# Attention feeding two mixture-of-experts layers: a chunk's normalized rows are stored in the chunk's own iteration

## The chip, the cores and the metric

The kernel runs on one core of a Trainium2 chip. The metric is the device time of one execution in microseconds (us). TensorE (PE), VectorE (DVE), ScalarE (ACT) and GpSimd (POOL) each work through their own queue in order; SyncE (SP) issues most of the transfers, also in order.

## The reference

Decayed linear attention runs over a sequence of 768 positions (2 batches, 8 heads, width 64), and its 1536 rows of 512 numbers go through two mixture-of-experts layers with 8 experts each. Cut to what matters here:

```python
for t in range(S):
    state = gamma * state + einsum('bhd,bhe->bhde', k[:, :, t], v[:, :, t])
    y[:, :, t] = scale * einsum('bhd,bhde->bhe', q[:, :, t], state)
x = y.transpose(0, 2, 1, 3).reshape(B * S, H * D)
logits = x @ w_gate
expert_idx = argmax(logits, axis=1)        # first layer: one expert per row
gate_w = softmax(logits)[expert_idx]
# each expert takes its rows in order, up to its capacity
out[i] = gate_w[i] * (relu(disp @ w1) @ w2)[expert_idx[i], pos[i]]
# second layer: rows are given to experts greedily by logit, 192 to an expert
out[mask] = relu(x[mask] @ w1[e]) @ w2[e]
```

## The kernel before, in words

Attention is computed in 12 chunks of 128 positions (NCH = 12; six per batch, NCB = 6), in a loop over j from 0 to 10 with chunk 11 written out behind it. The order of each engine's work is the order in which the code is written. One iteration j holds, in this order:

- the loads of k and v of chunk j+2 (`load_kv`, tile kv, L121) and of q and k transposed of chunk j+3 (`load_qk`, tile qk, L117), 512 KB each, on the SP queue. Each tile has three buffers, so a load waits until the chunk three before has been used up. In iterations 0, 1, 8 and 9 an expert weight tile is also asked for (`issue`, tile wst, L195, 512 KB, four buffers);
- `decay(j + 1)`: GpSimd multiplies k of chunk j+1 by powers of the decay (kv, L255; not for the last chunk of a batch) and q likewise (qd, L258; not for the first chunk of a batch);
- `values(j)`: TensorE forms the chunk's outputs from the running state U and qd (L279) and from the masked scores AM and v (L283); ScalarE copies them out as xT (L286), with positions along the free axis;
- `keep(j - 1)`, which the change moves (L328 to L340): from the sum of squares ss of a chunk's rows, three small VectorE steps (`pow2`, tile p, L229 to L232) make a power-of-two scale; ScalarE copies the rows from PSUM, scaled, into xo (L334); GpSimd adds a small number to the softmax sum se (g, L337), VectorE takes its reciprocal (L338), GpSimd writes the product with the inverse scale into the last column of xo (L339), and SP stores the tile to the DRAM tensor xd (L340, 256.5 KB);
- `place(j - 1, j - 2)`: positions of chunk j-1's rows within their experts (plc on TensorE, L346; jv and oa on VectorE, L350 and L353; ob on GpSimd, L355) and the slot numbers of chunk j-2 (`dispatch`, acc on VectorE, L372);
- in iterations 5 to 8 a load of a quarter of one expert's second weights (`wide_load`, tiles wbh and wbl, L184, 512 KB);
- `state(j)`: TensorE adds to the running state (ya, L296), VectorE scales it into U (L298); `scores(j + 1)`: TensorE (B, L265) and the mask multiply on VectorE (AM, L269);
- `rows_mm(j)`: TensorE turns xT into rows and adds the gate logits (tile R, L306). R has one PSUM buffer, so this matmul waits until the rows of chunk j-1 have been read, by xo last of all;
- `gate(j)`: on VectorE lg, m, dl, jv, rv, oh, ohs (L313 to L326), one behind the other; on ScalarE the squares (L319, which give ss) and the exponentials (L322, which give se);
- `fill(FT[j])`: that many weight splits. For each, ScalarE makes the high half of 512 columns of a weight tile (wah, L215) and VectorE the rest (wal, L220). When a tile of two splits is done, the next one is asked for on the SP queue.

In iteration 9 (NA = 9) the slots of chunks 0 to 8 are turned into row numbers idx, and at the start of iteration 10 GpSimd gathers the rows of two experts from xd (L393), which wait for the stores of chunks 0 to 8. The code for chunk 11 also transposes the first gathered rows (`x_split`, L409), stores the remaining chunks and gathers the rest. After it come the experts of both layers, whose lines the change does not touch. The number of splits per iteration is fixed:

```python
FT = (0, 2, 2, 2, 2, 2, 3, 1, 1, 1, 0, 0, 0, 0, 1, 0)
```

Of the kernel before, what the change touches and what calls it, by code (L numbers as in the profile page):

```python
# [89 lines left out]
def moe_chain(ctx, tc, qk, kv, wg, w1, w2, cap, wg2, w21, w22, mt, tq, tb, pv, out):  # L90
# [24 lines left out]
    def load_qk(j):  # L115
        QK[j] = qkv.tile([128, 2, KD, C], F32, name="qk")
        SP.dma_start(QK[j].rearrange("p a h t -> p (a h t)"), _dap(qk, j * 128 * 2 * DM, [[2 * DM, 128], [1, 2 * DM]]))  # L117

    def load_kv(j):
        KV[j] = qkv.tile([128, 2, H, D], F32, name="kv")  # L120
        SP.dma_start(KV[j].rearrange("p a h d -> p (a h d)"), _dap(kv, j * 128 * 2 * DM, [[2 * DM, 128], [1, 2 * DM]]))  # L121
# [58 lines left out]
    def wide_load(i, h):  # L180

        if not h:
            W["b", i] = [w16.tile([128, 4, DM], F32, name="wb" + x) for x in "hl"]
        SP.dma_start(W["b", i][h // 2][:, h % 2 * 2:h % 2 * 2 + 2],  # L184
                     _dap(w2, i * DM * F + h * 256 * DM, [[DM, 128], [128 * DM, 2], [1, DM]]))

    def issue():

        if not todo:
            return  # L190
        nm, i, h = todo.pop(0)
        src = ((w1, w2) if i < E else (w21, w22))[nm == "b"]
        kk, ff = ((KD, F), (KF, DM))[nm == "b"]
        st = wst.tile([128, 1024], F32, name="wst")
        SP.dma_start(st.rearrange("p (k f) -> p k f", k=kk // 4),  # L195
                     _dap(src, (i if i < E else (i + ROT) % E) * DM * F + h * DM * F // 4, [[ff, 128], [128 * ff, kk // 4], [1, ff]]))
        staged.append([st, nm, i, h, 0])

    def fill(n, need=None, pool=False):

        while staged:
            p = staged[0]
            st, nm, i, h, s = p
            if need is not None:
                if turn.index((nm, i)) > turn.index(need):
                    return
            elif n <= 0 or i > done[nm] + 3:
                return
            n -= 1
            if h == 0 and s == 0:  # L210
                W[nm, i] = tuple(w16.tile([128, 4096], F16, name="w" + nm + x)
                                 for x in "hl")
            o = h * 1024 + s * 512
            hi, lo = (t[:, o:o + 512] for t in W[nm, i])
            A.activation(hi, st[:, s * 512:(s + 1) * 512], AF.Copy, scale=WS)  # L215
            if pool:
                A.activation(st[:, s * 512:(s + 1) * 512], st[:, s * 512:(s + 1) * 512], AF.Copy, scale=WS)
                G.tensor_tensor(lo, st[:, s * 512:(s + 1) * 512], hi, OP.subtract)
            else:
                V.scalar_tensor_tensor(lo, st[:, s * 512:(s + 1) * 512], WS, hi, op0=OP.mult, op1=OP.subtract)  # L220
            p[4] += 1
            if p[4] == 2:
                staged.pop(0)
                issue()

    def pow2(ss, rows=128, k=1):

        t = wk.tile([128, 3, k], I32, name="p2" + str(k))
        V.tensor_scalar(t[:rows, 0], ss.bitcast(I32), 1, 0x7F800000, op0=OP.logical_shift_right,  # L229
                        op1=OP.bitwise_and)  # L230
        V.tensor_scalar(t[:rows, 1], t[:rows, 0], -1.0, float(193 << 23), op0=OP.mult, op1=OP.add)
        V.tensor_scalar(t[:rows, 2], t[:rows, 0], float(61 << 23), None, op0=OP.add)  # L232
        return t[:rows, 1].bitcast(F32), t[:rows, 2].bitcast(F32)
# [16 lines left out]
    def decay(j):  # L250

        c = j % NCB
        if c < NCB - 1:
            x = KV[j][:, 0]
            G.tensor_tensor(x, x, tkt[:, c, :, None].to_broadcast([128, H, D]), OP.mult)  # L255
        if c:
            QD[j] = wk.tile([128, KD, 128], F32, name="qd", tag="qT")
            G.tensor_tensor(QD[j], QK[j][:, 0], tqt, OP.mult)  # L258
# [15 lines left out]
    def values(j):  # L274
        b, c = divmod(j, NCB)
        p = ps.tile([128, KD, 128], F32, name="C1")
        for h in range(KD if c else 0):
            for s in range(2):
                P.matmul(p[s * 64:(s + 1) * 64, h, :], U[s * 64:(s + 1) * 64, h, :], QD[j][s * 64:(s + 1) * 64, h, :],  # L279
                         start=h == 0, stop=False, skip_group_check=True)  # L280
        for h in range(KD):
            for s in range(2):
                P.matmul(p[s * 64:(s + 1) * 64, h, :], KV[j][:, 1, 2 * h + s, :], AM[j][s][:, h, :],  # L283
                         start=not c, stop=True, skip_group_check=True)
        XT[j] = wk.tile([128, KD, 128], F32, name="xT")
        A.activation(XT[j], p, AF.Copy)  # L286
# [22 lines left out]
    def gate(j):  # L309

        pv = RW[j][:, :, :272].rearrange("p b (d c) -> p b d c", d=2)
        lg = wk.tile([128, E], F32, name="lg")
        V.tensor_reduce(lg, pv[:, :, :, 128:].rearrange("p b d e -> p e b d"), AX.XY, OP.add)  # L313
        m = wk.tile([128, 1], F32, name="m")
        V.tensor_reduce(m, lg, AX.X, OP.max)
        dl = wk.tile([128, E], F32, name="dl")
        V.tensor_scalar(dl, lg, m, None, op0=OP.subtract)
        ss = wk.tile([128, 1], F32, name="ss")
        A.activation(junk.rearrange("p (b d c) -> p b d c", b=2, d=2), pv[:, :, :, :128], AF.Square, accum_out=ss)  # L319
        ex = wk.tile([128, E], F32, name="ex")  # L320
        se = wk.tile([128, 1], F32, name="se")
        A.activation(ex, dl, AF.Exp, accum_out=se)  # L322
        V.scalar_tensor_tensor(jv, dl, 0.0, w8, op0=OP.is_ge, op1=OP.mult)
        V.tensor_reduce(rv[:, j:j + 1], jv, AX.X, OP.max)
        V.tensor_scalar(oh[:, j, :], w8, rv[:, j:j + 1], None, op0=OP.is_equal)
        V.tensor_tensor(ohs[:, j + 1, :], ohs[:, j, :], oh[:, j, :], OP.add)  # L326
        SS[j] = ss, se

    def keep(j):

        ss, se = SS[j]
        sc, inv = pow2(ss)
        xh = qkv.tile([128, XR], F32, name="xo", tag="g1")
        A.activation(xh[:, :DM].rearrange("p (b d c) -> p b d c", b=2, d=2),  # L334
                     RW[j][:, :, :272].rearrange("p b (d c) -> p b d c", d=2)[:, :, :, :128], AF.Copy, scale=sc)
        g = wk.tile([128, 1], F32, name="g")
        G.tensor_scalar(g, se, 1e-9, None, op0=OP.add)  # L337
        V.reciprocal(g, g)  # L338
        G.tensor_scalar(xh[:, DM:DM + 1], inv, OUT1, g, op0=OP.mult, op1=OP.mult)  # L339
        SP.dma_start(xd[j * 128:(j + 1) * 128, :], xh)  # L340
# [27 lines left out]
    def dispatch(j, sm):  # L368
        oa, ob = OH[j]
        for i in range(2):  # L370
            P.matmul(sm[:, i * E:(i + 1) * E], oa[:, i * 128:(i + 1) * 128], ob, start=True, stop=True)
        V.tensor_tensor(acc, acc, sm, OP.add)  # L372
# [18 lines left out]
    def gather(src, row, ix, key, e, i, n):  # L391
        t = qkv.tile([128, row], F32, name="xg", tag="g" + str(i))
        G.indirect_dma_start(out=t[:n], out_offset=None, in_=src,  # L393
                             in_offset=bass.IndirectOffsetOnAxis(ap=ix[:n, i * E + e:i * E + e + 1], axis=0))
        XG[key, i] = t
# [68 lines left out]
    for j in range(NCH - 1):  # L464
        if j + 2 < NCH:
            load_kv(j + 2)
        if j + 3 < NCH:
            load_qk(j + 3)
        if j in (0, 1, 8, 9):
            issue()  # L470
        decay(j + 1)
        if j == NA + 1:
            for e in range(2):
                gather(xd[:NA * 128, :], XR, idx, e, e, 0, 128)
        values(j)
        if j:
            keep(j - 1)
            place(j - 1, j - 2 if 1 < j != NA + 1 else None)
        if 5 <= j < 9:
            wide_load(0, j - 5)  # L480
        if j == NA:
            off = shift()
        state(j)
        scores(j + 1)
        if j == NA:
            dispatch(NA - 1, ps.tile([128, NQ], F32, name="dsp", tag="T", bufs=2))
            V.tensor_scalar(idx, acc, -1.0, 0.0, op0=OP.add, op1=OP.max)
        rows_mm(j)
        gate(j)
        fill(FT[j])  # L490
    j = NCH - 1
    values(j)
    x_split(0, (0, 128), tag="T")
    rows_mm(j)
    keep(j - 1)
    place(j - 1, j - 2)
    gate(j)
    l1(0, 0, 128, 0, 2, FT[11])
# [855 lines left out]
```

## Time and profile before

| | us |
|---|---|
| median of three runs | 472.17 |
| lowest, highest | 466.65, 477.76 |
| profiled execution | 465.31 |
| span of its profile | 463.5 |

The profile is one execution. Its span runs from the first instruction to the last; 1.8 us of the execution's time lie around it. Engine shares of the span: TensorE 88%, VectorE 66%, ScalarE 56%, GpSimd 27%. Rows of the timeline give the start, the duration, the engine and line, what is written from what, how many instructions a row merges, and in brackets how long the engine stood idle before it and on what. "SPq" is the SP queue's issue of a transfer.

### The profile page before, as it was taken

The page shows a single profiled execution, that of the slowest core. Times are in us where ns is not written, and L with a number is a line of the kernel's source. Part 1 is how long each engine was busy: PE and PEld are TensorE (multiplying, and loading weights), DVE is VectorE, ACT ScalarE, POOL GpSimd, SP SyncE. Part 2 cuts the span into 40 slices and gives each one's busy share as a digit, 9 for nine tenths or more (in the row PEclk, how much of TensorE's full clock was granted, in tenths as well). Part 3 has the DMA queues.
Part 4 walks back from the last instruction along what each step waited for, and adds up shares of the span by engine and source line. Part 5 has one row for each costly group of instructions (what it writes and reads, how often), then busy time and mean ns, then how long its engine had stood idle before and what let it go on. Part 6 is the DMA issues. An engine that isn't in the chain of part 4 may idle for free.

```text
span 463.5 us, 13188 instructions
## 1 busy us (share of the span) xinstructions
PE 407.4 (88%) x5398; PEld 383.2 (83%) x5398; DVE 304.9 (66%) x795; ACT 258.6 (56%) x571; POOL 124.2 (27%) x189
## 2 busy tenths in 40 slices
PE   6989688789899999999999769997899899999960
PEld 4767577789899999999999649997789789999960
DVE  2799787648789888878778666741279487872100
ACT  1345434447778786867866355331477677873310
POOL 1652544260020221302111056524111222111120
PEclk9899979999999999999999967999799999999995
DMA  9999996347899989888876435202178978971010
GB/s 202 395 313 266 367 330 212 134 150 248 283 292 289 311 275 285 259 293 269 268 245 188 128 112 181 92 3 59 69 250 272 299 236 297 302 240 36 24 49 5
DMA packets 42181, 98.83 MB, mean 213 GB/s; under 512 B 8896, under 2 KB 9280, under 8 KB 42112
## 3 DMA queue, kind: packets, MB, share of 16 engines
q1 hardware_dynamic: 35808, 84.31, 56.7%
q0 software_dynamic: 4608, 13.50, 9.1%
q8 instruction: 44, 0.72, 0.6%
q10 hardware_dynamic: 1696, 0.09, 0.4%
q14 instruction: 25, 0.20, 0.2%
HBM read 87.94 MB, written 9.95 MB: 211 GB/s over the span
## 4 chain that ended last, share of the span: by engine, by line
PE 52%; DVE 16%; DMA 15%; ACT 6%; issue 5%; POOL 2%; SPq 0%; POOLq 0%; ACTq 0%; DVEq 0%
DMA wst<-in_moe_w_dram 8%; PE T L440 7%; PE T L442 6%; PE T L441 6%; PE yps L551 6%; PE yps L550 6%; PE yps L552 6%; DVE wal L220 4%; DMA kv<-in_kv_dram 3%; DVE wbl L220 3%; PE xpt L409 3%; PE yps L546 3%; DMA xd<-xo 2%; ACT wbh L215 2%; DMA L<-yd 1%
## 5 line engine op out<-in xcount | busy, mean ns | idle before, releaser
L440 PE MATMUL T<-xsh,wah 128*128 128x216 f16 (+4 forms) x672 | 135.6, 233 | 4.6 <-DVE hl L457 2.8
L441 PE MATMUL T<-xsl,wah 128*128 128x216 f16 (+4 forms) x672 | 135.4, 233 | 0.0
L442 PE MATMUL T<-xsh,wal 128*128 128x216 f16 (+4 forms) x672 | 135.3, 233 | 0.0
L551 PE MATMUL yps<-hl,wbh 128*128 128x216 f16 (+3 forms) x544 | 116.0, 237 | 2.1 <-issue 1.7
L550 PE MATMUL yps<-hh,wbh 128*128 128x216 f16 (+3 forms) x544 | 116.0, 237 | 1.0 <-issue 1.0
L552 PE MATMUL yps<-hh,wbl 128*128 128x216 f16 (+3 forms) x544 | 116.0, 237 | 0.9 <-issue 0.9
L220 DVE SCALAR_TENSOR_TENSOR wal<-wst,wah 128x512 f16<-128x512 f32 x125 | 82.2, 702 | 16.7 <-ACT wah L215 13.5
L220 DVE SCALAR_TENSOR_TENSOR wbl<-wst,wbh 128x512 f16<-128x512 f32 x119 | 78.5, 698 | 15.7 <-ACT wbh L215 13.6
L215 ACT ACTIVATE wah<-wst 128x512 f16<-128x512 f32 x128 | 72.9, 622 | 8.6 <-DMA wst<-in_moe_w_dram 8.5
L215 ACT ACTIVATE wbh<-wst 128x512 f16<-128x512 f32 x120 | 69.3, 624 | 5.9 <-DMA wst<-in_moe_w_dram 5.9
L441 PEld LDWEIGHTS <-wah 128*128 128x128 f16 x672 | 66.0, 99 | 5.8 <-issue 5.5
L440 PEld LDWEIGHTS <-wah 128*128 128x128 f16 x672 | 66.1, 99 | 0.1
L442 PEld LDWEIGHTS <-wal 128*128 128x128 f16 x672 | 66.0, 99 | 0.0
L551 PEld LDWEIGHTS <-wbh 128*128 128x128 f16 x544 | 52.6, 98 | 3.0 <-issue 2.8
L552 PEld LDWEIGHTS <-wbl 128*128 128x128 f16 x544 | 52.6, 98 | 2.5 <-issue 2.3
L457 DVE SCALAR_TENSOR_TENSOR hl<-T,hh 128x432 f16<-128x432 f32 (+4 forms) x64 | 32.0, 502 | 33.2 <-ACT hh L451 32.3
L550 PEld LDWEIGHTS <-wbh 128*128 128x128 f16 x544 | 52.8, 99 | 0.7
L451 ACT ACTIVATE hh<-T 128x432 f16<-128x432 f32 (+4 forms) x76 | 32.9, 435 | 32.6 <-PE T L442 32.2
L583 POOL DMA_INDIRECT yd<-yr,sidx x16 | 16.5, 1032 | 118.3 <-ACT yr L635 90.6
L583 POOL DMA_INDIRECT out_dram<-orow,ixo x16 | 15.2, 951 | 99.3 <-ACT orow L1015 91.3
L570 ACT ACTIVATE yT<-yps 128x384 f32<-128x384 f32 (+2 forms) x20 | 7.9, 393 | 33.3 <-PE yps L552 21.5
L422 DVE TENSOR_TENSOR xsl<-xpt,xsh 128x432 f16<-128x432 f32 (+4 forms) x32 | 14.9, 498 | 15.5 <-ACT xsh L416 15.4
(256 smaller groups left out, 672.4 us busy)
## 6 DMA issues: line engine op xcount, KB each, us to landing
wst<-in_moe_w_dram SPq DMA_DIRECT2D x124, 512.0 KB
qk<-in_qk_dram SPq DMA_DIRECT2D x12, 512.0 KB
kv<-in_kv_dram SPq DMA_DIRECT2D x12, 512.0 KB
xd<-xo SPq DMA_DIRECT2D x12, 256.5 KB
wbh<-in_moe_w_dram SPq DMA_DIRECT2D x2, 512.0 KB
wbl<-in_moe_w_dram SPq DMA_DIRECT2D x2, 512.0 KB
pvt<-in_pv_dram SPq DMA_DIRECT2D x3, 192.0 KB
mt<-in_mt_dram SPq DMA_DIRECT2D x2, 256.0 KB
```

The costliest lines, as they stand in the source:

```text
L215: A.activation(hi, st[:, s * 512:(s + 1) * 512], AF.Copy, scale=WS)
L220: V.scalar_tensor_tensor(lo, st[:, s * 512:(s + 1) * 512], WS, hi, op0=OP.mult, op1=OP.subtract)
L422: V.tensor_tensor(lo, pd, hi, OP.subtract)
L440: P.matmul(p[:, s, c0:c1], wh[:, d, fs], xh[:, d, c0:c1], start=d == 0, stop=False)
L441: P.matmul(p[:, s, c0:c1], wh[:, d, fs], xl[:, d, c0:c1], start=False, stop=False)
L442: P.matmul(p[:, s, c0:c1], wl[:, d, fs], xh[:, d, c0:c1], start=False, stop=d == KD - 1)
L451: A.activation(hh, p[:, :, c0:c1], AF.Relu)
L457: V.scalar_tensor_tensor(hl, p[:, :, c0:c1], 0.0, hh, op0=OP.max, op1=OP.subtract)
L550: P.matmul(p[:, s, c0:n], wh[:, f, dsl], hh, start=f == 0, stop=False)
L551: P.matmul(p[:, s, c0:n], wh[:, f, dsl], hl, start=False, stop=False)
L552: P.matmul(p[:, s, c0:n], wl[:, f, dsl], hh, start=False, stop=f == KF - 1)
L583: w = G.indirect_dma_start(out=dst, out_offset=bass.IndirectOffsetOnAxis(ap=ap, axis=0), in_=src, in_offset=None)
```

## The change

`keep(j)` is called at the end of iteration j, between `gate(j)` and `fill(FT[j])`, for j from 0 to 10; before, `keep(j - 1)` was called in iteration j, behind `values(j)`, and for chunk 10 behind `rows_mm(11)`. `keep(11)` stays where it was.

```diff
         values(j)
         if j:
-            keep(j - 1)
             place(j - 1, j - 2 if 1 < j != NA + 1 else None)
...
         rows_mm(j)
         gate(j)
+        keep(j)
         fill(FT[j])
     j = NCH - 1
     values(j)
     x_split(0, (0, 128), tag="T")
     rows_mm(j)
-    keep(j - 1)
     place(j - 1, j - 2)
     gate(j)
```

On ScalarE, in the program's iterations 1 and 2 (R is the chunk's rows, p its scale, C the outputs of the chunk behind it, ind a scratch tile that takes the squares), before:

```order
L322 ACTIVATE ex,se<-dl 128x8
L215 ACTIVATE wah<-wst 128x512 x2
L286 ACTIVATE xT<-C_365 128x512
L334 ACTIVATE xo<-R_330,p_384 128x512
L319 ACTIVATE ind_155,ss<-R_428 128x512
```

and now:

```order
L322 ACTIVATE ex,se<-dl 128x8
L334 ACTIVATE xo<-R_330,p_350 128x512
L215 ACTIVATE wah<-wst 128x512 x2
L286 ACTIVATE xT<-C_376 128x512
L319 ACTIVATE ind_155,ss<-R_428 128x512
```

The scaled copy xo has moved ahead of both high halves wah and of the next chunk's xT.

On VectorE, at the end of iteration 1 (the scale steps p and the reciprocal g of chunk 1, then the splits):

```order
 L326 TENSOR_TENSOR ohs<-ohs,oh 128x8
+L229 TENSOR_SCALAR p_350<-ss 128x1
+L231 TENSOR_SCALAR p_350<-p_350 128x1
+L232 TENSOR_SCALAR p_350<-p_350 128x1
+L338 RECIPROCAL g<-g 128x1
 L220 SCALAR_TENSOR_TENSOR wal<-wst,wah 128x512 x2
-L229 TENSOR_SCALAR p_384<-ss 128x1
-L231 TENSOR_SCALAR p_384<-p_384 128x1
-L232 TENSOR_SCALAR p_384<-p_384 128x1
-L338 RECIPROCAL g<-g 128x1
 L372 TENSOR_TENSOR acc<-acc,plc 128x16
 L350 SCALAR_TENSOR_TENSOR jv,posv<-plc,oh 128x8
```

The four steps have moved from behind the splits to ahead of them.

On the queue of GpSimd, around iteration 2 (kv and qd are the decay multiplies of chunk 3, g and xo GpSimd's part of a stored row, ob a step of place), before:

```order
L255 TENSOR_TENSOR kv<-kv,tbt 128x512
L258 TENSOR_TENSOR qd<-qk,tqt 128x512
L337 TENSOR_SCALAR g<-se 128x1
L339 TENSOR_SCALAR xo<-p_384,g 128x1
L355 TENSOR_SCALAR ob<-oh,id_152 128x8
```

and now:

```order
L337 TENSOR_SCALAR g<-se 128x1
L339 TENSOR_SCALAR xo<-p_350,g 128x1
L255 TENSOR_TENSOR kv<-kv,tbt 128x512
L258 TENSOR_TENSOR qd<-qk,tqt 128x512
L355 TENSOR_SCALAR ob<-oh,id_152 128x8
```

Chunk 1's part of the row has moved ahead of chunk 3's multiplies. The SP queue keeps its cycle of store, wst, kv and qk, with the store of chunk j-1 where that of chunk j-2 stood ahead of the loads of iteration j.

## Rows read from the trace of the kernel before

**Rows 1.** Busy time by stage: PE, PEld, DVE, ACT, POOL, then PEclk, DMA share, GB/s.

```profile
20.00:45.00 25.00, 21.60 (x311) 18.57 (x308) 23.57 (x86) 12.88 (x33) 10.70 (x20) 1.00 1.00 302
45.00:73.00 28.00, 21.37 (x281) 18.37 (x281) 22.35 (x78) 12.10 (x31) 13.44 (x20) 0.88 1.01 346
```

**Rows 2.** The chain of waits, 33 to 45 us: start, us, what.

```profile
34.29 6.26 DMA kv<-in_kv_dram
...
40.69 1.05 POOL kv L255
...
43.65 0.28 POOL xo L339
...
44.20 5.06 DMA xd<-xo
```

**Rows 3.** Timeline: the matmul L306 of chunk 1 and of chunk 11.

```profile
20.76 1.19 PE L306 MATMUL R<-idw,xT 128*128 128x136 f32 x8
...
85.21 1.19 PE L306 MATMUL R<-idw,xT 128*128 128x136 f32 x8
```

**Rows 4.** Timeline, 33 to 40 us: gate, splits, scale steps and the next mask multiply.

```profile
33.47 1.28 DVE L269 TENSOR_TENSOR AM<-B,mt 128x512 f32<-128x512 f32 x2
33.49 1.28 POOL L258 TENSOR_TENSOR qd<-qk,tqt 128x512 f32<-128x512 f32 x1
...
34.66 0.18 DVE L313 TENSOR_REDUCE lg<-R 128x8 f32<-128x32 f32 x1
...
35.71 1.14 ACT L215 ACTIVATE wah<-wst 128x512 f16<-128x512 f32 x2
...
36.00 0.17 DVE L326 TENSOR_TENSOR ohs<-ohs,oh 128x8 f16<-128x8 f16 x1
36.36 1.29 DVE L220 SCALAR_TENSOR_TENSOR wal<-wst,wah 128x512 f16<-128x512 f32 x2 [0.19 <-ACT wah L215]
...
37.57 0.15 DVE L229 TENSOR_SCALAR p<-ss 128x1 int32<-128x1 int32 x1
37.76 0.15 DVE L231 TENSOR_SCALAR p<-p 128x1 int32<-128x1 int32 x1
...
37.95 0.69 ACT L334 ACTIVATE xo<-R,p 128x512 f32<-128x512 f32 x1 [0.61 <-DVE p L231]
37.96 0.15 DVE L372 TENSOR_TENSOR acc<-acc,plc 128x16 f32<-128x16 f32 x1
...
38.15 0.27 POOL L339 TENSOR_SCALAR xo<-p,g 128x1 f32<-128x1 f32 x1 [1.95 <-DVE g L338]
...
38.77 1.28 DVE L269 TENSOR_TENSOR AM<-B,mt 128x512 f32<-128x512 f32 x2
...
39.96 0.18 DVE L313 TENSOR_REDUCE lg<-R 128x8 f32<-128x32 f32 x1
```

**Rows 5.** Timeline: VectorE steps beside GpSimd's multiplies, at 23 and at 55 us.

```profile
22.77 1.13 DVE L323 SCALAR_TENSOR_TENSOR jv<-dl,w 128x8 f32<-128x8 f32 x1
...
54.69 3.81 DVE L220 SCALAR_TENSOR_TENSOR wal<-wst,wah 128x512 f16<-128x512 f32 x3 [0.20 <-ACT wah L215]
54.81 1.47 POOL L255 TENSOR_TENSOR kv<-kv,tbt 128x512 f32<-128x512 f32 x1 [2.96 <-DMA kv<-in_kv_dram]
...
56.25 1.71 POOL L258 TENSOR_TENSOR qd<-qk,tqt 128x512 f32<-128x512 f32 x1
```

**Rows 6.** Waits of VectorE, 0 to 95 us: us in total, times, longest.

```profile
DVE g L338 <- POOL g L337: 4.5, 2, 2.4
```

**Rows 7.** Timeline of L306 in iteration 6, and two windows (PEclk third from the end).

```profile
59.53 2.18 PE L306 MATMUL R<-idw,xT 128*128 128x136 f32 x8 [3.23 <-ACT xo L334]
...
58.00:59.00 1.00, 0.00 (x0) 0.00 (x0) 0.97 (x8) 0.21 (x1) 0.54 (x2) 0.73 0.96 360
...
65.00:66.00 1.00, 1.00 (x24) 0.69 (x22) 0.72 (x9) 0.48 (x1) 0.32 (x2) 0.85 1.05 367
```

**Rows 8.** Timeline of the SP queue: a kv load.

```profile
45.66 0.40 SPq L121 DMA_DIRECT2D kv<-in_kv_dram  x1
```

## The prediction

> **What bounds the kernel now.** Read the windows by stage first, then the chain of waits, then the timeline of single iterations. The change lies in the attention loop, which runs from about 15 to 88 us of the 463.5; what follows is a chain behind the gathers of its rows, so I take a shift of its end as a shift of the whole. From 20 to 73 us all three of VectorE, TensorE and the DMA engines look full: VectorE is busy 23.57 of 25.00 us in the first part and 22.35 of 28.00 in the second, the DMA share is 1.00 and 1.01 at 302 and 346 GB/s [rows 1]. The chain of waits goes from one kv load (6.26 us to landing) to GpSimd's multiply of it, to GpSimd's part of a stored row, and from there to the store [rows 2]. So the loop is tied to two things at once: a ring through VectorE and ScalarE, and a ring through the SP queue, where a kv load stands behind a store that itself needs GpSimd.
>
> The measure is the step from one row-turning matmul (L306) to the next. The first in full stride starts at 20.76 us, the last, of chunk 11, at 85.21 [rows 3]: ten periods in 64.45 us. The cleanest period is the one from lg at 34.66 to lg at 39.96, 5.30 us with two weight splits in it [rows 4]. 64.45 is 11 us more than ten of these. The surplus is made of VectorE waiting for GpSimd's multiplies [rows 5], of two reciprocals that wait for GpSimd's g (4.5 us in all, longest 2.4) [rows 6], and of a stretch at half clock [rows 7].
>
> **The change part by part.** No instruction is added or taken out. Per chunk move: three small VectorE steps and the reciprocal, one ScalarE copy (xo, 0.69 us), two GpSimd steps, and one store on the SP queue.
>
> *ScalarE and VectorE.* Until now ScalarE makes the splits' high halves (wah) while VectorE is still in the gate, so VectorE goes from the gate to wal after 0.19 us of waiting, and the p steps come behind. Now xo stands ahead of wah, and xo needs the p steps, which need the whole gate on VectorE's queue. Counted from the start of lg, by [rows 4]: the last gate step starts at 1.34 and takes 0.17, so p at 1.51; 0.19 to the second p, 0.19 on to xo: 1.89; xo 0.69: 2.58; from wah to the first wal 0.65: 3.23; two wal 1.21 (36.36 to 37.57): 4.44; acc to AM 0.81: 5.25; AM to the next lg 1.19: 6.44. That is 1.14 longer than 5.30. The cover that goes is the gate: wah ran beside it, and now VectorE stands idle from the reciprocal to 3.23. A period with one split is 0.61 shorter, 5.83, one with three 7.05; the period of iteration 10, with none, stays at 5.30. Iterations 1 to 5 have two splits, 6 has three, 7 to 9 one: 32.2 + 7.05 + 17.5 + 5.3 = 62.0 us without any waits for GpSimd.
>
> *What goes.* The matmul L306 no longer waits for xo, but its input xT now comes behind xo and both wah, so that is worth nothing by itself. The reciprocal no longer stands behind the next chunk's decay multiplies, and at iteration 10 no longer behind the two gathers: 4.5 us of stalls that the 62.0 does not contain. At the end, chunk 10's p steps and reciprocal leave the chain in front of the last gate: 0.39 (37.57 to 37.96 in [rows 4]).
>
> *GpSimd against VectorE.* This is the largest uncertain term. While GpSimd multiplies kv (1.05 us alone [rows 2]) or qd (1.28 [rows 4]), VectorE steps with both inputs in SBUF wait: three wal take 3.81 us instead of 3 times 0.61, a wait of 1.91 and a price of 0.96 where the small jv takes 1.13 instead of 0.17 [rows 5]. The mask multiply AM, 1.28 us, is not touched by a qd started 0.02 us behind it [rows 4]. In the new order GpSimd is free for the next multiplies after its part of the row, which starts 0.39 behind the second p (37.76 to 38.15) and takes 0.27 [rows 4]: 1.70 + 0.39 + 0.27 and 0.1 to the next, at about 2.45 after lg. If the load is there by then, kv runs to 3.5, holds the first wal by 0.26, and qd holds the second by its 1.28: 1.5 per pair. Six chunks (3, 4, 7 to 10) have the pair, three a single one (0.49 for the qd of chunks 5 and 11, 0.26 for the kv of chunk 6). Is the load there? The store goes out 0.55 after the start of GpSimd's part (43.65 to 44.20) [rows 2], the kv load 1.46 behind the store with two loads between, of which one now stands ahead of the store (44.20 [rows 2] to 45.66 [rows 8]), so about 1.0; it is issued 3.6 after lg, lands 6.3 [rows 2] to 9.1 us later (45.66 to the multiply at 54.81 [rows 5]) and so, with a period of 7, between 3 and 6 after the next lg. Partly it falls on wal, partly on AM, where it costs nothing. I take three quarters, 1.15 for a pair, which is near the lower row, and 0.9 for the singles: 6.9 + 0.9 = 7.8. The ends: nothing, and 1.91 for each pair with 1.24 for the singles, 12.7.
>
> The Trainium skill, "SBUF — State Buffer", Who interferes with whom, says that a VectorE step with two SBUF inputs and a GpSimd step that reads SBUF shut each other out for a whole instruction, and one with a single SBUF input is left alone. With the full 1.5 on six pairs and 1.24 for the singles that would be 10.2 instead of 7.8, and a result 2.4 us higher than mine. The trace agrees on wal (3.81) and on AM (1.28); what it can't show is where the multiplies fall in the new order.
>
> *The SP queue.* Each kv and qk load now stands behind the store of the chunk just gated, where before it stood behind that of the chunk before. The loads go out some 4 to 5 us later against the arithmetic, and the backlog of the DMA engines shrinks. In iterations 5 to 8 a chunk moves four loads of 512 KB and a store of 256.5, 2.36 MB, which at 346 GB/s [rows 1] takes 6.8 us, 27.3 for the four. My periods there are 25.2 without waits and about 30 with them, so the DMA engines bind only if the waits vanish; then 2.1 us come back. The ring through the queue (1.0 from store to kv load, up to 9.1 to landing, 2.3 of multiplies, about 1 for GpSimd's small steps, 0.55 to the next store but one) is 14.0 over two iterations, 7.0 each, just under my mean period of 7.2 with waits, so I put it at nothing.
>
> *Sum.* 62.0 + 7.8 = 69.8 against 64.45: 5.4 longer, less 0.39 at the end: **5.0 us slower**. Low end: 62.0 + 2.1 − 64.45 − 0.4, or 0.7 us faster. High end: 62.0 + 12.7 − 64.45 − 0.4, or 9.9 slower. The profiled execution took 465.31, so 470.3 in its place; the three runs have a median of 472.17, 6.9 above it, so I give 477.2 against that median.
>
> **The rivals.**
> *The waits hide.* The multiplies land under AM and the matrix work, and the stalls that go pay for the longer ring: −0.7 us, 471.5. For it: the qd in [rows 4] costs nothing, and a load that lands late moves its multiplies under AM. Against it: a late load delays the row's store, so the loads settle where they just arrive, and that is beside wal.
>
> *The clock falls again and again.* This one ends more than 2% slower. In the kernel before TensorE stood idle for 3.23 us before L306 at 59.53, and the granted clock was half of 2.4 GHz from about 58.4 to 65.3 us (0.73 in the slice from 58, 0.85 in that from 65) [rows 7]; L306 then took 2.18 instead of 1.19. TensorE has some 5.2 us of work in a period (42.97 of 53 us [rows 1], of a mean period of 6.45); in new ones of 7 or more it idles 2 to 2.6 us in every one, cut in two by the waits for U and for xT. If these pieces join to one as long as that before 59.53, the clock can fall in every second or third period. One fall costs, as an estimate, 1.7 us (6.9 us at half speed cost 3.5 us of its work, of which I count half as lying beside VectorE). Three falls are 5.2 on top of 5.0: 10.2 slower, 482.4; five are 13.6. Against it: TensorE's order puts the matmuls of values (L279, L283) between the two waits, so no piece should pass 2 us. It decides once a period's idling is one piece.
>
> **How the numbers follow.** Forecast 0.68, with a range of its own from 473 to 482; waits hidden 0.20; clock 0.12. The measurement can tell about 2%, 9.4 us. Slower by more: the clock's 0.12, and a twentieth of the forecast (all pairs at 1.91): 0.15. Faster by more would need the ring through xo not to be there: 0.03. Within 2%: 0.82. The range goes from 468 (hidden waits, and a median of runs that lie 11 us apart) to 485 (three or four falls of the clock).
>
> **What would show it.** Right: ten periods of L306 in about 70 us; wal starting 3.2 us behind lg, with ScalarE's wah behind xo, and VectorE's waits for wah of more than 1 us in each of nine periods instead of 0.19; the wait of the reciprocal for g gone. Wrong: wah beside the gate, or wal undisturbed in all periods (the hidden case), or a granted clock under 0.9 in several places between 20 and 75 us (the clock), or an unchanged start of the last L306 near 85.

## The result, and the profile after

The changed kernel is slower, by less than 2%: 474.22 us (median of 4 runs, 472.05 to 478.7) against 470.43 for the kernel before on the same chip (4 runs, 466.65 to 477.76), a ratio of 1.0114 with an interval of 1.0070 to 1.0159. That is 5.4 us (3.3 to 7.5) on 470.43. The ratio is of fast runs alone, so it is not quite that of the two medians, which stand 3.8 us apart. The forecast was 5.0 us slower, "within 2%", 477.2 us.

| | before | after |
|---|---|---|
| profiled execution, us | 465.31 | 474.18 |
| its span | 463.5 | 472.4 |
| L306 of chunk 1 and of chunk 11 start at | 20.76, 85.21 | 20.42, 92.67 |
| ten periods between them | 64.45 | 72.25 |
| the first nine of them (to chunk 10) | 58.88 | 66.72 |

The two profiled executions stand 8.9 us apart, more than the ratio says: that of before took 465.31, 5.1 below its own median, that of after stands at its median. A difference of one or two us between single executions is therefore not to be built on; one that a run with a single edit takes away again is.

Busy time by stage of the kernel after (the columns of [rows 1]; the loop is longer, so the second window ends later):

```profile
20.00:45.00 25.00, 20.88 (x278) 17.80 (x274) 20.56 (x70) 10.12 (x28) 11.21 (x16) 0.93 0.89 249
45.00:79.00 34.00, 23.46 (x311) 19.91 (x310) 27.09 (x93) 14.07 (x36) 16.34 (x23) 0.95 0.98 301
```

In [rows 1] VectorE was busy 23.57 of the first 25 us with 86 instructions; now it is 20.56 with 70, and the DMA share has fallen from 1.00 to 0.89. Neither is full any longer in this stretch. The matmuls that answer to [rows 3], from the timeline:

```profile
20.42 1.19 PE L306 MATMUL R<-idw,xT 128*128 128x136 f32 x8
...
92.67 1.09 PE L306 MATMUL R<-idw,xT 128*128 128x136 f32 x8
```

One iteration of the kernel after, 21 to 30 us, from lg to lg, to be held beside [rows 4]:

```profile
21.81 0.17 DVE L313 TENSOR_REDUCE lg<-R 128x8 f32<-128x32 f32 x1
...
23.59 0.69 ACT L334 ACTIVATE xo<-R,p 128x512 f32<-128x512 f32 x1 [0.64 <-DVE p L231]
...
23.79 0.27 POOL L339 TENSOR_SCALAR xo<-p,g 128x1 f32<-128x1 f32 x1 [0.53 <-DMA kv<-in_kv_dram]
...
24.14 1.04 POOL L255 TENSOR_TENSOR kv<-kv,tbt 128x512 f32<-128x512 f32 x1
...
24.18 1.14 ACT L215 ACTIVATE wah<-wst 128x512 f16<-128x512 f32 x2
...
24.83 2.58 DVE L220 SCALAR_TENSOR_TENSOR wal<-wst,wah 128x512 f16<-128x512 f32 x2 [1.14 <-ACT wah L215]
...
25.14 1.72 POOL L258 TENSOR_TENSOR qd<-qk,tqt 128x512 f32<-128x512 f32 x1
...
29.34 0.18 DVE L313 TENSOR_REDUCE lg<-R 128x8 f32<-128x32 f32 x1
```

ScalarE's wah, which in [rows 4] ran beside the gate, now comes behind xo, and VectorE stands idle for 1.14 us in front of wal, which starts 3.02 us behind lg. GpSimd's multiplies begin right behind its part of the row, so kv and qd run beside wal: two wal take 2.58 us where [rows 4] has 1.29. The chain of waits now runs through just these instructions up to 76.84 us, where it goes over to a weight load; one piece of it from 69 us on:

```profile
69.01 0.69 ACT xo L334
...
70.25 0.90 DVE wal L220
...
72.69 1.19 DVE AM L269 x2
...
75.60 0.69 ACT xo L334
```

The waits of the kernel after, 0 to 105 us (us in total, times, longest). The wait of the reciprocal for g, 4.5 us in [rows 6], is no longer among them:

```profile
DVE wal L220 <- ACT wah L215: 10.1, 9, 1.1
...
PE dsp L371 <- POOL ob L355: 3.2, 1, 3.2
...
PE xpt L409 <- DMA xg<-xd,idx: 1.8, 1, 1.8
```

The first is the forecast's, nine times. The other two are not in the forecast. That for ob makes the longest period, chunk 8 to chunk 9, 9.77 us. The timeline there:

```profile
77.78 1.13 POOL L255 TENSOR_TENSOR kv<-kv,tbt 128x512 f32<-128x512 f32 x1 [1.72 <-DMA kv<-in_kv_dram]
...
78.88 1.26 POOL L258 TENSOR_TENSOR qd<-qk,tqt 128x512 f32<-128x512 f32 x1
...
80.12 0.31 POOL L355 TENSOR_SCALAR ob<-oh,id 128x8 f16<-128x8 f16 x1
...
80.48 0.19 PE L371 MATMUL dsp<-ob,oa 128*128 128x8 f16 x2 [3.22 <-POOL ob L355]
...
80.53 2.02 PE L306 MATMUL R<-idw,xT 128*128 128x136 f32 x8
```

The kv load of chunk 10 is late; on GpSimd ob of chunk 8 stands behind the multiplies that wait for it; in iteration 9 TensorE needs this ob in front of L306 (the dispatch of chunk 8, on which the first gather's indices rest).

### The profile page after: what moved, and what is told of

Same layout as the page of the kernel before. It is cut to its first block, busy times and chain, and to the rows that moved or that the text cites. A ratio compares the mean times of both kernels' runs of the same rounds, so it can differ in the third digit from the quotient of the medians.

```text
span 472.4 us, 13182 instructions
## 1 busy us (share of the span) xinstructions
PE 410.3 (87%) x5398; PEld 384.6 (81%) x5398; DVE 310.1 (66%) x795; ACT 257.9 (55%) x571; POOL 128.0 (27%) x189
## 4 chain that ended last, share of the span: by engine, by line
PE 45%; DVE 21%; DMA 10%; issue 10%; ACT 8%; POOL 3%; SPq 0%; POOLq 0%; ACTq 0%; DVEq 0%
PE T L442 6%; PE T L440 6%; DMA wst<-in_moe_w_dram 6%; PE T L441 6%; PE yps L549 5%; PE yps L550 5%; PE yps L551 5%; DVE wal L220 5%; DVE wbl L220 4%; PE yps L545 2%; ACT wah L215 2%; PE xpt L409 2%; DVE AM L269 2%; DMA xg<-yd,ix 2%; DMA kv<-in_kv_dram 2%
## 5 line engine op out<-in xcount | busy, mean ns | idle before, releaser
L220 DVE SCALAR_TENSOR_TENSOR wal<-wst,wah 128x512 f16<-128x512 f32 x125 | 87.8, 745 | 28.1 <-ACT wah L215 24.6
L220 DVE SCALAR_TENSOR_TENSOR wbl<-wst,wbh 128x512 f16<-128x512 f32 x119 | 81.5, 724 | 17.3 <-ACT wbh L215 16.9
L319 ACT ACTIVATE ind<-R 128x512 f16<-128x512 f32 x12 | 7.2, 597 | 41.2 <-DVE lg L313 41.2
## 6 DMA issues: line engine op xcount, KB each, us to landing
xd<-xo SPq DMA_DIRECT2D x12, 256.5 KB
```

## The experiments

Three theories were set against each other. A: the scale steps and xo ahead of the splits hold up wah, and with it VectorE. B: the loads, which now stand behind the store of the chunk just gated, come late. C: the clock falls in the longer periods. All runs, each ratio against the kernel before in the same set of runs, and the loop as its profile shows it:

| kernel | ratio, interval | nine periods | ten |
|---|---|---|---|
| before | 1 | 58.88 | 64.45 |
| after | 1.0114, 1.0070 to 1.0159 | 66.72 | 72.25 |
| step behind the splits | 0.9965, 0.9918 to 1.0013 | 58.75 | 64.01 |
| store an iteration later | 1.0154, 1.0102 to 1.0205 | 62.68 | 70.97 |
| extra matmuls | 1.0077, 1.0036 to 1.0119 | 67.02 | 72.02 |
| after, no multiplies | – | 54.84 | – |
| before, no multiplies | – | 47.66 | – |
| after, ob early | 1.0129, 1.0062 to 1.0195 | 65.71 | 74.64 |
| step behind the splits, ob early | 0.9975, 0.9937 to 1.0013 | 60.18 | 64.86 |
| the same, gathers at once | 0.9929, 0.9880 to 0.9979 | 58.56 | 64.79 |
| the same, store later too | 0.9908, 0.9861 to 0.9955 | 53.29 | 64.36 |
| store later, gathers at once | 1.0030, 0.9991 to 1.0069 | 62.87 | 67.94 |
| before, g early | 1.0028, 0.9985 to 1.0071 | 61.61 | 66.10 |
| behind the splits, ob early, store later | 0.9861, 0.9819 to 0.9903 | 53.27 | 59.87 |

**The step behind the splits.** One line moves: everything stays in the chunk's own iteration, only the order against the splits is that of before.

```diff
         gate(j)
-        keep(j)
         fill(FT[j])
+        keep(j)
```

> The changed kernel with keep(j) still in its own iteration but behind the weight splits instead of ahead of them. If the splits pay (scale steps and xo ahead of wah): wal starts again about 1.7 us behind lg, the ten periods of L306 fall from 72.2 to 61 to 65 us, and the time is at or below that of the kernel before (ratio 0.98 to 1.00). If the loads pay (kv and qk behind the store of the chunk just gated): the store goes out later still, the periods stay at 70 to 74 and the ratio at 1.01.

Measured: ten periods 64.01 in place of 72.25, ratio 0.9965, with an interval that ends below where that of the changed kernel begins. From its timeline at 40 us, and the wait for ob that is left:

```profile
40.33 0.18 DVE L313 TENSOR_REDUCE lg<-R 128x8 f32<-128x32 f32 x1
...
41.38 1.14 ACT L215 ACTIVATE wah<-wst 128x512 f16<-128x512 f32 x2
...
42.03 1.29 DVE L220 SCALAR_TENSOR_TENSOR wal<-wst,wah 128x512 f16<-128x512 f32 x2 [0.19 <-ACT wah L215]
...
43.82 0.27 POOL L339 TENSOR_SCALAR xo<-p,g 128x1 f32<-128x1 f32 x1 [1.96 <-DVE g L338]
...
45.63 1.04 POOL L255 TENSOR_TENSOR kv<-kv,tbt 128x512 f32<-128x512 f32 x1 [1.54 <-DMA kv<-in_kv_dram]
...
73.87 0.19 PE L371 MATMUL dsp<-ob,oa 128*128 128x8 f16 x2 [3.72 <-POOL ob L355]
```

wal starts 1.70 behind lg, as in [rows 4]. A second thing is to be seen: GpSimd's part of the row (43.82) waits for VectorE's reciprocal, which stands with the p steps behind wal. So the multiplies, which stand behind it in GpSimd's queue, can't start before wal is over, and two wal take 1.29 us in each of the five periods that have two. The order of the two parts decides both what ScalarE does first and when GpSimd is let go. A holds.

**The store an iteration later.** The changed kernel, but the store is issued at its old place on the SP queue, behind the next iteration's loads.

```diff
+        if j < NCH - 1:
+            XH[j] = xh
+        else:
+            store(j, xh)
...
+    def store(j, xh):
         SP.dma_start(xd[j * 128:(j + 1) * 128, :], xh)
...
         if j:
+            store(j - 1, XH[j - 1])
             place(j - 1, j - 2 if 1 < j != NA + 1 else None)
...
     rows_mm(j)
+    store(j - 1, XH[j - 1])
     place(j - 1, j - 2)
```

> The changed kernel with the store alone issued at its old place on the SP queue, in the next iteration, so that the kv and qk loads stand ahead of it again; all else as changed. If the splits pay: ten periods of 69 to 72 us, the wait of the kv multiply for its load gone or small, ratio 1.005 to 1.012. If the loads pay: ten periods of 63 to 66, ratio about 1.00.

Measured: the waits of VectorE for wah are unchanged (10.1 us in 9), nine periods fall by 4.0 us to 62.68, but the last one takes 8.29 in place of 5.53, and the ratio is 1.0154, above what either theory gave, with an interval that overlaps that of the changed kernel. The timeline at the end of the loop shows what takes 2.8 of the 4.0 us back:

```profile
79.10 0.17 DVE L495 TENSOR_SCALAR idx<-acc 128x16 int32<-128x16 f32 x1
...
82.98 1.43 POOL L401 DMA_INDIRECT xg<-xd,idx  x1 [0.18 <-issue]
...
90.11 1.11 PE L417 MATMUL xpt<-idw,xg 128*128 128x128 f32 x4 [3.68 <-DMA xg<-xd,idx]
```

The indices are there at 79.10, the gather goes out 3.9 us later, behind GpSimd's g, its part of the row and the multiply of qd, and its rows reach TensorE 7.1 us after that. So B is a part of the loop's loss, and hardly of the total as long as the gathers stand where they do (the run with both edits, below, bears on this).

**Extra matmuls.** Eight warm-up matmuls behind each L306, so that TensorE has less idle time.

```diff
         rows_mm(j)
+        if j:
+            warm(8)
         gate(j)
```

> The changed kernel with eight idle matmuls (256 columns each, about 1.1 us, result unused) behind L306 in iterations 1 to 10, where TensorE otherwise waits. If the clock pays: no window under 0.9 between 20 and 90 us, ten periods of 67 to 69 us, 3 to 5 us back of the changed kernel's time. If the splits pay: the clock holds but the periods stay at 71 to 72, since VectorE sets them; a gain of 1 us or less.

Measured: ten periods 72.02, ratio 1.0077, which the intervals don't tell from 1.0114. Windows of this run:

```profile
25.00:50.00 25.00, 22.41 (x312) 18.83 (x309) 19.55 (x72) 11.18 (x30) 11.47 (x17) 1.00 0.80 237
50.00:80.00 30.00, 24.29 (x323) 20.25 (x321) 24.21 (x80) 12.99 (x34) 14.17 (x19) 1.00 0.97 302
```

The granted clock (third from the end) is 1.00 from 25 to 80 us. The seven periods from chunk 1 to chunk 8, which lie in this stretch but for the first 1.3 us, take 49.74 us; in the changed kernel, with two falls of the clock among them, they take 50.34. So these falls do not set the periods, and C is dropped as the cause of the loop's length. Later the clock falls here too (0.69 from 85 to 90 us), so the third fall of the changed kernel, from 80 us on, is not tested by this run. The added matmuls take some 1.04 us of TensorE's time in an iteration, beside VectorE's work; that they cost a little of what the clock gives back is not excluded.

**Without the decay multiplies, after and before.** A pair: both kernels without GpSimd's multiplies of kv and qd from chunk 3 on, so that only the order of the other work is left.

```diff
         c = j % NCB
+        if 3 <= j:
+            QD[j] = QK[j][:, 0]
+            return
         if c < NCB - 1:
```

> The changed kernel without GpSimd's decay multiplies from chunk 3 on (kv and q are used as loaded, so the rows, the routing and all times behind the attention loop are others; only the loop is read). By the sum of the prediction the periods without waits are 6.44 us with two splits, 7.05 with three, 5.83 with one: ten periods of about 62 to 63 us, wal 3.0 to 3.3 us behind lg, two wal in 1.3 us. If the loads pay instead, the periods stay near 72 us, with TensorE waiting for kv or qk.

> The kernel before without the decay multiplies of kv and qd from chunk 3 on (this part of the computation is left out, so only the attention loop is read and not the whole time). It is the partner of the changed kernel without the same multiplies, whose nine periods from chunk 1 to chunk 10 were 54.84 us. Theory A (the scale steps and the scaling of the row stand ahead of the weight splits and set the period wherever GpSimd does not): the same nine periods fall to about 45 us, some 1.1 us less in each, the first wal starts about 1.9 behind lg in place of 3.02, and xo no longer stands between lg and wah. Theory B (the loads, which stand behind the store of the chunk just gated, set the period): the loads of the kernel before are not behind that store, so its periods also fall, but the first wal would stand as late behind lg as before the change of order, and the sum would be limited by waits for kv. If neither holds, and the multiplies are what the change lengthens, the nine periods stay within 2 us of 54.84.

Measured: nine periods 54.84 (forecast 56.7) and 47.66 (expected some 45). The tenth (8.05 and 14.81), in which the gathers fall, is not read, since the rows and the routing are others in these two. One iteration of the changed order, then one of the order before, each from its timeline:

```profile
34.15 0.18 DVE L316 TENSOR_REDUCE lg<-R 128x8 f32<-128x32 f32 x1
...
35.94 0.69 ACT L337 ACTIVATE xo<-R,p 128x512 f32<-128x512 f32 x1 [0.64 <-DVE p L231]
...
37.17 1.29 DVE L220 SCALAR_TENSOR_TENSOR wal<-wst,wah 128x512 f16<-128x512 f32 x2 [1.14 <-ACT wah L215]
...
40.40 0.18 DVE L316 TENSOR_REDUCE lg<-R 128x8 f32<-128x32 f32 x1
```

```profile
34.00 0.18 DVE L316 TENSOR_REDUCE lg<-R 128x8 f32<-128x32 f32 x1
...
35.06 1.14 ACT L215 ACTIVATE wah<-wst 128x512 f16<-128x512 f32 x2
...
35.71 1.29 DVE L220 SCALAR_TENSOR_TENSOR wal<-wst,wah 128x512 f16<-128x512 f32 x2 [0.20 <-ACT wah L215]
...
39.30 0.18 DVE L316 TENSOR_REDUCE lg<-R 128x8 f32<-128x32 f32 x1
```

6.25 from lg to lg against 5.30, with wal 3.02 and 1.71 behind lg: the order alone costs 7.2 us in nine periods, and waits for loads have next to no part in it (one of 1.1 us, GpSimd's for a kv load, in the changed order). What the multiplies (with what waits for them) add on top is 66.72 − 54.84 = 11.9 after and 58.88 − 47.66 = 11.2 before. So in these two executions the whole difference, 7.84, is the order's 7.18 and 0.66 more. The multiplies cost about the same in both; they only stop other instructions.

**The kernel before with g early.** Only g (a small GpSimd step) and its reciprocal on VectorE, here `recip(j)`, move into the chunk's own iteration, behind the splits; the rest stays as before.

```diff
         gate(j)
         fill(FT[j])
+        recip(j)
```

> The kernel before with only g and its reciprocal moved into the chunk's own iteration, behind the splits; the scale steps, the row's scaling, its last column and the store stay an iteration later. The forecast counted the two waits of the reciprocal (4.5 us) as the one thing that the change removes. If that is right, the wait goes, ten periods fall from 64.45 to 60 to 62, and the ratio is 0.990 to 0.995. Rival (the wait is hidden by the GpSimd multiplies or followed by another wait for the same late load): the wait goes but ten periods stay within 1 us of 64.45, ratio 0.998 to 1.001.

Measured: no gain, ratio 1.0028, and ten periods of 66.10, longer than either expectation. VectorE's wait for g falls from 4.5 to 0.7 us. From the timeline:

```profile
31.73 1.04 POOL L255 TENSOR_TENSOR kv<-kv,tbt 128x512 f32<-128x512 f32 x1
...
31.83 3.18 DVE L220 SCALAR_TENSOR_TENSOR wal<-wst,wah 128x512 f16<-128x512 f32 x2 [0.19 <-ACT wah L215]
...
32.73 1.72 POOL L258 TENSOR_TENSOR qd<-qk,tqt 128x512 f32<-128x512 f32 x1
```

With g out of the way GpSimd goes from g straight to the multiplies, and these now stop wal (3.18 us for two). The 4.5 us of reciprocal waits were no loss that could simply be taken out: what stood behind the multiplies waited, what now stands beside them waits instead.

**ob early, in the changed kernel.** To price the wait that the forecast had not seen; `early_ob(j)` is GpSimd's ob of chunk j, which `place(j)` then uses.

```diff
         gate(j)
+        early_ob(j)
         keep(j)
```

> The changed kernel, with GpSimd's ob of a chunk computed in that chunk's own iteration, right behind the gate, where before it stood a full iteration later behind the multiplies. Theory (the missed term is the wait of TensorE for ob of chunk 8, behind the late multiplies of kv 10): the wait of dsp for ob (3.2 us) goes, the period from chunk 8 to chunk 9 falls from 9.77 to 6.5 to 7.0, the ten periods from 72.25 to about 69.3, and the whole time by 3 us, to a ratio of 1.003 to 1.008 with the kernel before. Rival (the late load of kv 10 holds this period in any case, through the multiply and what follows it): the period stays above 9 and the ratio at 1.011.

Measured: the period from chunk 8 to chunk 9 falls from 9.77 to 6.25, as expected, and the ratio is 1.0129: nothing is won. The period before it takes 9.64 in place of 7.52, beside a half-clock stretch (granted clock 0.82 in the window from 65 to 70 us, 0.50 from 70 to 75), and at the end of the loop TensorE waits 3.92 us for the gathered rows instead of 1.79. The expectation for the total failed; that these two follow from the wait that went, and are not one execution's luck, was not tested.

**ob early, with the step behind the splits.**

```diff
         gate(j)
-        keep(j)
         fill(FT[j])
+        early_ob(j)
+        keep(j)
```

> The changed kernel with the step placed behind the weight splits of its own iteration, and ob computed ahead of it. Theory: to the 64.01 us of ten periods that the step behind the splits gave, the removed wait for ob (3.7 us) gives back some 3 to 3.5, so ten periods of about 60.7 and a ratio of 0.988 to 0.992. Rival (what the wait hid is only uncovered: the load of kv 10 or the clock): ten periods stay above 63 and the ratio at 0.996.

Measured: ratio 0.9975 and ten periods 64.86, no gain over 0.9965 and 64.01; the rival had it right. The timeline shows the wait's successor:

```profile
73.54 1.04 POOL L255 TENSOR_TENSOR kv<-kv,tbt 128x512 f32<-128x512 f32 x1 [4.12 <-DMA kv<-in_kv_dram]
...
74.54 1.26 POOL L258 TENSOR_TENSOR qd<-qk,tqt 128x512 f32<-128x512 f32 x1
...
75.85 1.97 PE L279 MATMUL C<-qd,U 64*64 64x128 f32 x16 [3.60 <-POOL qd L258]
```

The load of kv 10 is late, and what waited for ob behind its multiply (3.72 us) waits now for qd behind it (3.60). At this one place the root is the load, as B has it.

**The gathers at once.** As the last, with the two gathers right behind idx in iteration 9, not in iteration 10 behind g, xo and qd.

```diff
         decay(j + 1)
-        if j == NA + 1:
-            for e in range(2):
-                gather(xd[:NA * 128, :], XR, idx, e, e, 0, 128)
...
             V.tensor_scalar(idx, acc, -1.0, 0.0, op0=OP.add, op1=OP.max)
+            for e in range(2):
+                gather(xd[:NA * 128, :], XR, idx, e, e, 0, 128)
```

> As the kernel before it in this call (step behind the splits, ob early), and the two gathers of the first expert are issued right behind idx in iteration 9, not an iteration later behind g, xo and qd on GpSimd. Theory (TensorE's wait for the gathered rows and the late start of the experts hang on the gathers' place on GpSimd): gathers within 1 us of idx, no wait of xpt for xg, the second gather of the experts 1 to 2 us earlier against the last row-turning matmuls, ratio 0.983 to 0.989. Rival (the gathers' 2 to 2.5 us on GpSimd delay g, xo and qd of the last iterations, and the experts start when the last chunk's store is done in any case): the last two periods grow by 1 to 2 us and the ratio stays within 0.002 of the kernel without this edit.

Measured: ratio 0.9929, between the two expectations, and by the intervals not told from the 0.9975 without this edit. TensorE no longer waits for the gathered rows, but the gather starts 5.4 us behind idx (75.17 to 80.56), not 1: for the last 3.42 of these GpSimd waits in it for the store of chunk 8, and g, xo and qd wait behind.

**The store later as well.** To take the late load away: the edits of the last kernel and the store at its old place on the SP queue, as in the run above.

```diff
         if j:
+            store(j - 1, XH[j - 1])
             place(j - 1, j - 2 if 1 < j != NA + 1 else None)
```

> The step behind the weight splits of its own iteration, ob early, the gathers right behind idx, and the store of a chunk's rows issued an iteration later, behind that iteration's loads. Theory B for the end of the loop (the loads that queue behind the store come 4 to 5 us later, and the one of kv 10 then ends the wait of iteration 9 or 10, whichever instruction stands behind it): kv 10 is no longer waited for, the step that without this edit took 8.8 to 11 us near chunk 9 or 10 falls to 6 to 7, nine periods from 58.6 to 60.2 down to about 55, and the ratio with the kernel before to 0.978 to 0.986. Rival (the DMA engines are full from 45 to 80 us in any case, so the place in the queue decides nothing): nine periods stay at 58 or more and the ratio at 0.993.

Measured: kv 10 is not waited for any more, the period from chunk 8 to 9 is 5.25 and nine periods are 53.29, better than expected (this profiled execution took 469.47, the median is 467.27). But the last period takes 11.07, and the ratio is 0.9908, not the 0.978 to 0.986 expected. The timeline names the cause:

```profile
75.79 1.19 POOL L406 DMA_INDIRECT xg<-xd,idx  x1 [6.94 <-DMA xd<-xo]
...
79.65 1.27 POOL L258 TENSOR_TENSOR qd<-qk,tqt 128x512 f32<-128x512 f32 x1
```

GpSimd stands 6.94 us in the gather until the store of chunk 8 has landed, and qd of chunk 11, which TensorE needs (it waits 5.28 us), stands behind.

**The old split order with both later edits.** The changed kernel, step ahead of the splits, with the gathers at once and the store later, its line as in the last diff.

```diff
             V.tensor_scalar(idx, acc, -1.0, 0.0, op0=OP.add, op1=OP.max)
+            for e in range(2):
+                gather(xd[:NA * 128, :], XR, idx, e, e, 0, 128)
         rows_mm(j)
         gate(j)
         keep(j)
         fill(FT[j])
```

> The changed kernel (the step ahead of the weight splits) with the gathers right behind idx and the store issued an iteration later, behind the loads. Theory A says that what is left against the kernel before is the place of the scale steps and of the row's scaling ahead of the splits: nine periods at about 62 to 63, some 4 us more than the kernel before's 58.88, the last period back at 5.5 to 6 in place of 8.29, and a ratio of 1.004 to 1.010. Rival (the loads and the gathers carry most of the 1.1%): nine periods at 59 or less, ratio 1.000 or below.

Measured: nine periods 62.87, as A has it, the last 5.07; the ratio is 1.0030, just under the 1.004 expected, with an interval of 0.9991 to 1.0069. Loads and gathers carry a part of the 1.1%, then; in the first nine periods the old order still costs 9.6 us against the four-place kernel above (53.29), which also has ob early.

**Three places.** The kernel with the four edits, with the gathers back at their place in iteration 10, behind qd.

```diff
         decay(j + 1)
+        if j == NA + 1:
+            for e in range(2):
+                gather(xd[:NA * 128, :], XR, idx, e, e, 0, 128)
...
             V.tensor_scalar(idx, acc, -1.0, 0.0, op0=OP.add, op1=OP.max)
-            for e in range(2):
-                gather(xd[:NA * 128, :], XR, idx, e, e, 0, 128)
```

> As the kernel with four places changed, but the two gathers are back at their place in iteration 10, behind the last multiply of qd: the step behind the splits, ob early, the store behind the next iteration's loads. Theory (GpSimd's wait of 6.9 us for the store of chunk 8, with g, xo and qd behind it, was what the early gathers cost there): qd of chunk 11 is ready before C asks for it, the last period falls from 11.07 to 8 or less, nine periods stay at 53 to 54, the gathers start at once behind idx's last releaser without a wait for the store of over 1.5 us, and the ratio with the kernel before is 0.980 to 0.988. Rival (the store's landing sets the end of the stage wherever the gathers stand): the first matmul that takes gathered rows starts no earlier against chunk 1 than in the four-place kernel, and the ratio stays at 0.989 to 0.993.

Measured: as expected in each point, and 1.4% faster than the kernel before, with an interval (0.9819 to 0.9903) below one and below that of the change: 462.11 us against 467.69, ratio 0.9861. In its timeline the gather no longer waits for the store, and two of the last matmuls of the loop stand at:

```profile
73.92 1.19 POOL L406 DMA_INDIRECT xg<-xd,idx  x1 [0.18 <-issue]
...
78.97 0.91 PE L422 MATMUL xpt<-idw,xg 128*128 128x128 f32 x4 [2.65 <-DMA xg<-xd,idx]
...
79.68 2.02 PE L306 MATMUL R<-idw,xT 128*128 128x136 f32 x8
```

With L306 of chunk 1 at 19.81 us that is ten periods of 59.87, 4.6 us less than in the kernel before. Its DMA share is 1.01 from 20 to 45 us, and its granted clock 1.00 from 15 to 75. Whether it needs ob early was not run.

## Why the prediction was right, and where it was off

*The mechanism.* Right in each of its points. wah stands behind xo; wal starts 3.02 us behind lg (forecast 3.23); VectorE waits for wah in nine periods, 10.1 us in all, 1.12 each on average, where the forecast had over 1 us in each (one of them, with three splits, was 0.93); the reciprocal's wait is gone; ten periods came out longer, 72.25 for "about 70". That it is the order against the splits is shown by the run that undoes it alone, 64.01, and by the pair without multiplies, 7.2 us apart.

*The ScalarE and VectorE term.* 56.7 us for the first nine periods (five of 6.44, one of 7.05, three of 5.83); 54.84 without multiplies. The single periods fit: three of the two-split periods took 6.26, the three-split one 7.04, two of the one-split ones 5.65 and 5.61. The error is mostly in the first, 5.38: L306 of chunk 1 starts 1.32 us ahead of its lg and the later ones 2.20, so this period is 0.9 shorter, though from lg to lg it has 6.26 as well.

*GpSimd against VectorE.* The mis-sized term: 7.8, against 11.9 measured. It counts the multiplies of chunks 3 to 11, which stand beside the splits of iterations 1 to 9, so all of it falls in the first nine periods. What was measured has two parts. 3.3 is the period from chunk 8 to 9 (9.77 against 6.46 without multiplies), which is no stop of VectorE (wal takes 0.69 there) but TensorE's wait for ob. The other 8.6 lie in eight periods. There my three quarters give 6.65 (7.8 less the 1.15 of one pair), and the full price gives 8.7 (five pairs of 1.5, and the singles' 1.24). So the full price comes out in sum, mine was too low, and the wait for ob was missing altogether. (The wait of three wal, 1.91, is right against the 1.90 that three take without multiplies; "3 times 0.61", as the forecast writes, is 1.83.) That VectorE and GpSimd stop each other, as the Trainium skill has it ("SBUF — State Buffer", Who interferes with whom), this trace agrees with on both sides: at 24.83 two wal took 2.58 in place of 1.29 with kv and qd beside them, and that qd 1.72 in place of 1.28.

*What goes.* "4.5 us of stalls that the 62.0 does not contain" is true of the sum, yet as a gain by itself it was not to be had: with g early and nothing else, the same multiplies stop wal, and the ratio is 1.0028.

*The SP queue.* "So I put it at nothing" is the step that did not hold. That the loads come later was right, but it was averaged over the ring. The store's place is worth 4.0 us in the nine periods of the changed kernel (62.68 with the store later), spread over them: only 1.3 fall on the period from chunk 8 to 9 (8.51 for 9.77), for which the load of kv 10 is late. With the step behind the splits it is 5.5 (58.75 against 53.27, ob early too), and there 5.2 fall on that one period (10.48 against 5.25). Part of it came back at the end, through the gather, which the prediction did not follow past the loop.

*Rivals.* "The waits hide" would have had ten periods near 64; they did not. "The clock falls again and again" was right that it falls and wrong in what it costs: windows of the kernel after

```profile
35.00:40.00 5.00, 3.80 (x36) 3.24 (x36) 3.81 (x15) 1.92 (x6) 1.90 (x5) 0.66 0.85 275
50.00:55.00 5.00, 4.99 (x54) 4.15 (x55) 3.62 (x14) 3.09 (x8) 2.00 (x4) 0.66 0.98 321
80.00:85.00 5.00, 4.52 (x40) 4.04 (x41) 3.59 (x17) 1.49 (x6) 0.97 (x5) 0.66 0.85 308
```

show three falls in the loop, the number for which I had added 5.2 us; a clock under 0.9 in several places between 20 and 75 us was my sign of that rival, and two of them lie there. What was to decide it, a period's idling in one piece, was there only for the third: TensorE idled 3.22 us before the matmul at 80.48, and at most 1.6 in one piece before the other two. With the clock held at 1.00 over the stretch of the first two, the seven periods there were 0.6 us shorter (49.74 for 50.34).

*The total.* 5.0 us slower against 5.4 by the ratio. In the profiled executions the loop lengthened by 7.8 us, not by the 5.4 of the sum, but the one that I started from lay 5.1 us below the median of its kernel, so this pair overstates the change. Which of its waits a usual execution of the kernel before has more of was not looked into; in the nine periods one term was 1.9 us too high and the other 4.1 too low. That the sum met the ratio so closely is in part luck.

## What to carry to other kernels

When a step is moved on several in-order queues, ask of each queue what it now stands ahead of: here two engines were let go at the wrong moment, ScalarE (xo ahead of wah) and GpSimd (its multiplies beside wal), and one line further down both were right. A wait that a trace shows is not a gain to be had: follow the late thing behind it, since what stands behind it next may wait in its place (here ob, then qd, behind one load). And an edit that helps the loop can lose it again at the loop's exit: read the exit's own queue, here the gather behind a store.

## What the runs showed that was not expected

The granted clock fell twice in the changed kernel behind idle pieces that were short. Before the first fall TensorE had idled 1.32 us before C at 28.37 and 1.60 before C at 36.20, in periods of some 7.5 us, and the clock was 0.66 over the window from 35 to 40; before the second no piece was longer than 1.37. In the forecast it took a single piece of about 3 us, as in [rows 7] and as before the third fall. From the timeline:

```profile
28.37 1.09 PE L279 MATMUL C<-qd,U 64*64 64x128 f32 x16 [1.32 <-DVE U L298]
...
36.20 1.90 PE L279 MATMUL C<-qd,U 64*64 64x128 f32 x16 [1.60 <-DVE U L298]
```

In the four-place kernel (the store later as well), a store of 256.5 KB that was issued at 66.77, with the DMA share at 1.02 to 1.06 from 60 to 70 us, had landed only when GpSimd's wait for it ended at 75.79, 9.0 us later; the one of [rows 2] took 5.06.
